# Attention with a gated MLP on one core: the table that sets the sequence of 2,462 steps is set anew

## The chip, the core and the metric

The kernel runs on one core of one Trainium2 chip. The core has TensorE (PE in the profile) for matrix products, VectorE (DVE), ScalarE (ACT) and GpSimd (POOL) for everything element by element, and SyncE (SP), which here only issues DMAs. Each engine works through its own list of instructions in order; semaphores hold an instruction until what it reads or overwrites is ready. The metric is the device time of one execution in microseconds (us), the median of several runs.

## The reference, cut to what matters

```
attention:  q, k, v are [4, 12, 448, 64]                       # batch, heads, tokens, width
    scores = q @ k.T / 8, causal mask, minus the row's maximum
    attn   = exp(scores) / (sum(exp(scores)) + 1e-9)
    x      = attn @ v, heads side by side                      # [4, 448, 768]
gated MLP, for each batch:
    h      = relu(x @ w_in)                                    # [448, 1024]
    u, v   = h[:, :512], h[:, 512:]
    v_n    = (v - mean(v)) / sqrt(var(v) + 1e-6)
    v_s    = w_spatial @ v_n + b_spatial                       # over the tokens
    out    = (u * v_s) @ w_out                                 # [448, 768]
```

w_in and w_out arrive as 64-bit floats, the other inputs as 32-bit floats.

## The kernel before, in words

**Tiling.** The 48 heads are taken two at a time: 24 pairs, six to a batch. Products that must be exact to more than 16 bits are made of three 16-bit products: every operand is split into a high part (`h`) and a low part (`l`), and a chain multiplies high by high, high by low and low by high.

**The steps.** For the first ten pairs ("wide" pairs) `qk_prepare` turns q and k on TensorE (L763 for pair 0, L789 for the others) into a PSUM bank, and ACT or DVE copies the bank to `qkT` (L772, L774, L810, L812). `wide` makes the scores in float32 (L979), DVE takes mask and row extreme in one step (L1017), ACT the exponential with its sum (L1027), DVE the reciprocal (L1038, L1046), one of POOL, ACT or DVE the scaling (`scaled_copy`: L496 is its form on DVE, L498 on ACT, L500 on POOL), TensorE turns the result (L1066) and ACT or DVE copies it (L1090, L1092). `attend` multiplies by v into the one bank `px` (L1300), and ACT and DVE take it out as high and low part of `xT` (L1317, L1322): until L1322 has read `px`, the next pair's L1300 waits. The other 14 pairs scale and split q and k first (L577 or L579 a sum of squares, on ACT or DVE; L623 its total on TensorE; L500 and L532 the split), are turned by DMA, and make their scores from 16-bit parts (L1146, L1147, then L1157, L1169, L1183, L1191, L1258).

**Weights.** `prep_in` and `prep_out` load w_in and w_out, turn 64-bit words into 32-bit floats on DVE in three steps (`from_double`: L1335, L1341, L1346), and split them (L500, L532). `v_load` loads v.

**The MLP.** `ffn` of a batch makes all its products in chains of three matmuls (L1544): v's half of h (`wi` by `xT`, four tiles of tokens), its evacuation (L1617), mean and variance (L1625, L1630, L1636, L1644 on POOL, L1651), the norm (L1661 on ACT or L1663 on POOL) and the split (`scaled_copy` and L1676) into `vn`; u's half (`xT` by `wi`); the spatial product (`wst` by `vn`), which needs `vn` of all four tiles; the gate (L1730, then L1564); and the output product (`wo` by `g`), evacuated by L496 or L498 and stored by L1782.

**What sets the order.** No scheduler runs. `Plan.add` collects 2,462 steps in program order, and three tables written into the file decide the rest: `ORDER` gives the sequence in which all steps are issued, and so each engine's list; `WHERE` gives the engine (A, P, D or S) of each step that can run on more than one; `FILLS` puts so many idle products (L714, 256 columns, into a bank that holds nothing) in front of a step on TensorE. Buffers are handed out in that sequence too, so that a buffer's number can differ while the work is the same. `Plan.run` also plays the sequence through with costs, for the length that it reports; these are not waits in the program. The lines of it that issue:

```python
for n in ORDER:
    op = self.ops[n]
    e = op.at_engine
    ...
    if e in op.lock:
        start = max(start, pool_end)
    if e == "POOL":
        start = max(start, dve_end)
    if e == "PE":
        last = op.cls
        if n in FILLS and (2, []) in free["pf"]:
            order += [(self.warm, e)] * FILLS[n]
    ...
    order.append((op, e))
```

Of the kernel before, what the change touches and what calls it, by code (L numbers as in the profile page):

```python
# [46 lines left out]
    15: 10, 17: 1, 19: 3, 21: 2, 158: 6, 160: 7,  # L47
# [4 lines left out]
    "AADAPPDAAPAPPPPPPAPPPPAADPAAPPDDAAPAAAAAPAAAPPADPAAAPAADDAPDPDDAAPDPPDADADAPADAADAADAAPDAAPPAAPPAAAAPDAAAAAPAP"  # L52
    "APAAAPAAPAADADDAAAAAPPAPPAAAAAAAAAPPADAAPAPAPPDAPPAADPPPPAAADPPAPPPPPADDAAAAAAAPPAAAADDPAPAPDAAADAAPPDDAAAAPAD"
    "DAPDAAADAADAAAAAAAPPAAPDSPDPAAAAAAPADAAAAAPAPAAPAPPAAAAAAPAAPSSAADDPPPPPPPAPPADAAPPAPAPDPPPAAADDAAAAAPPPPPPPPA"
    "AAPPPPAPDPAAAPPPPPPAAPADAPPDPPPAPAAPAPDDPDAPAAADAPPPDPPDAAAPAPPPPPAPPPADDAPPAPPPPPPDAADDAAAAAPPAAPPPPAAAPPADPS"
    "APAAPPPPPPSPPAAAPPPPPSAPADAPPPAPDAPPDDPADADPAAPPDADDDPPPAPDDAPADAAADAA"
)
ORDER = (
# [1788 lines left out]
```

## Time and profile before

| | us |
|---|---|
| median of 3 runs (lowest, highest) | 351.37 (351.15, 351.75) |
| the profiled execution: its time | 352.04 |
| its span, first to last instruction | 350.1 |
| TensorE busy, share of the span | 339.0, 97% |
| VectorE busy | 283.9, 81% |
| ScalarE busy | 273.5, 78% |
| GpSimd busy | 167.1, 48% |

The profile is one execution, in which every instruction has a start and a duration. Busy time of an engine is the union of its instructions' durations. Matmuls overlap: a matmul's duration is longer than the distance to the next one, so that the rate is read from the distance (a row of n matmuls, less one duration, divided by n - 1). A wait is the idle time of an engine in front of an instruction, put down to what ended last before it.

### The profile page before, as it was taken

To read this page: it belongs to the slowest core of one execution; us is meant where nothing else is said; L and a number is where in the kernel's file an instruction comes from. 1 tells how busy PE (TensorE), PEld (TensorE's weight loads), DVE (VectorE), ACT (ScalarE), POOL (GpSimd) and SP (SyncE) were. 2 spreads that over 40 slices of the span, in tenths; PEclk is the share of its full clock that TensorE was granted. 3 is DMA by queue.
4 is the path that set the end of the run, shared out by engine and by line. 5 is a ranking of instruction groups with operands and counts; after the bars stand their busy time and mean duration, and the time that the engine had idled before them with its cause. 6 is when DMAs were issued, how large, how long until landed. Compare 5 with 4: busy or idle time off the path is not lost.

```text
span 350.1 us, 8017 instructions
## 1 busy us (share of the span) xinstructions
PE 339.0 (97%) x2603; PEld 198.8 (57%) x2603; DVE 283.9 (81%) x1079; ACT 273.5 (78%) x747; POOL 167.1 (48%) x232
## 2 busy tenths in 40 slices
PE   7899998999999999999999999999999999999996
PEld 5556664655466565555565556654655665454563
DVE  4899999899999999997889988888999886263310
ACT  2798998999999999997997889899879676113112
POOL 3221962238535979662465665336788500033300
PEclk9999999999999999999999999999999999999999
DMA  7789938887876889998989979989887939500023
GB/s 176 167 223 215 278 69 210 213 197 203 161 180 172 146 170 180 180 206 186 178 192 181 173 158 176 228 187 185 130 128 146 162 81 166 153 2 0 2 87 93
DMA packets 160987, 55.49 MB, mean 158 GB/s; under 512 B 155249, under 2 KB 157106, under 8 KB 160946
## 3 DMA queue, kind: packets, MB, share of 16 engines
q1 hardware_dynamic: 160946, 54.99, 76.7%
q8 instruction: 20, 0.33, 0.4%
q14 instruction: 21, 0.17, 0.2%
HBM read 26.76 MB, written 5.51 MB: 92 GB/s over the span
## 4 chain that ended last, share of the span: by engine, by line
PE 46%; ACT 5%; DVE 5%; POOL 2%; issue 1%; ACTq 0%; DVEq 0%; POOLq 0%
PE pf L1544 37%; PE px L1300 5%; PE ps L1146 2%; PE ps L1147 2%; ACT ps L1169 2%; ACT junk L577 1%; DVE ps L1157 1%; DVE ln L1625 1%; ACT hv L1661 1%; POOL vn L1676 1%; ACT e L498 1%; DVE e L1258 1%; ACT hv L1617 0%; DVE junk L579 0%; ACT o L498 0%
## 5 line engine op out<-in xcount | busy, mean ns | idle before, releaser
L1544 PE MATMUL pf<-wi,xT 128*128 128x512 f16 (+1 forms) x360 | 62.4, 337 | 0.0
L1544 PE MATMUL pf<-xT,wi 128*128 128x448 f16 x288 | 59.5, 353 | 0.2 <-ACT hv L1617 0.2
L1169 ACT ACTIVATE ps<-ps,sm 128x384 f32<-128x384 f32 (+4 forms) x98 | 45.3, 464 | 10.0 <-DVE sm L1157 8.5
L1258 DVE SCALAR_TENSOR_TENSOR e<-ps,sm,e 128x256 f16<-128x256 f32 (+4 forms) x98 | 45.8, 505 | 5.4 <-ACT e L498 4.5
L1544 PE MATMUL pf<-wo,g 128*128 128x384 f16 x288 | 49.2, 326 | 0.2 <-ACT o L498 0.2
L1157 DVE CUSTOM_DVE_ANT_0 ps<-ps,mask,sc 128x256 f32<-128x256 f32 (+4 forms) x98 | 46.8, 507 | 1.5 <-ACT et L1090 0.2
L498 ACT ACTIVATE e<-ps,sm 128x256 f16<-128x256 f32 (+4 forms) x98 | 42.6, 509 | 3.3 <-DVE sm L1191 1.3
L532 POOL TENSOR_TENSOR qks<-qk,qks 112x512 f16<-112x512 f32 x28 | 33.5, 1204 | 20.1 <-DVE qks L496 10.6
L1544 PEld LDWEIGHTS <-wi 128*128 128x128 f16 x288 | 27.0, 98 | 27.0 <-issue 3.1
L1544 PEld LDWEIGHTS <-xT 128*128 128x128 f16 (+1 forms) x360 | 27.6, 102 | 23.7 <-issue 2.7
L1544 PEld LDWEIGHTS <-g 128*128 128x128 f16 (+1 forms) x288 | 27.7, 98 | 19.7 <-issue 1.1
L500 POOL TENSOR_SCALAR e<-e,sm 128x256 f32<-128x256 f32 (+3 forms) x33 | 17.1, 530 | 42.5 <-DVE sm L1046 13.5
L1027 ACT ACTIVATE e<-ps,sm 128x384 f32<-128x384 f32 (+3 forms) x70 | 34.2, 498 | 3.9 <-DVE sm L1017 2.3
L1544 PE MATMUL pf<-wst,vn 128*128 128x448 f16 (+1 forms) x176 | 35.6, 353 | 0.5 <-POOL vn L1676 0.5
L979 PE MATMUL ps<-qkT 64*128 64x256 f32 (+3 forms) x160 | 28.4, 446 | 2.1 <-ACT e L1027 1.6
L1544 PEld LDWEIGHTS <-vn 128*128 128x128 f16 (+1 forms) x176 | 16.6, 98 | 16.8 <-POOL vn L1676 1.4
L1644 POOL TENSOR_TENSOR ln<-ln,mhalf 128x1 f32<-128x1 f32 (+1 forms) x16 | 9.5, 591 | 34.8 <-DVE ln L1636 34.6
L1017 DVE CUSTOM_DVE_ANT_0 ps<-ps,e 128x128 f32<-128x128 f32 (+2 forms) x60 | 24.3, 448 | 2.1 <-PE ps L979 1.9
L1147 PE MATMUL ps<-qkT 128*64 128x256 f16 (+4 forms) x196 | 25.7, 285 | 0.0
L1066 PE MATMUL ps<-ident,e 128*128 128x128 f32 x160 | 24.1, 280 | 1.0 <-DVE e L496 0.6
L1146 PE MATMUL ps<-qkT 128*64 128x256 f16 (+4 forms) x196 | 24.2, 288 | 0.0
L1300 PE MATMUL px<-et,vs 128*64 128x448 f16 (+3 forms) x336 | 22.6, 275 | 0.1
(182 smaller groups left out, 710.1 us busy)
## 6 DMA issues: line engine op xcount, KB each, us to landing
wb<-in_moe_w_in_dram SPq DMA_DIRECT2D x12, 512.0 KB, 4.5
vnat<-in_v_dram SPq DMA_DIRECT2D x24, 192.0 KB, 4.2
out_dram<-o SPq DMA_DIRECT2D x9, 384.0 KB, 3.5
qk<-in_q_dram SPq DMA_DIRECT2D x14, 224.0 KB, 4.2
qk<-in_k_dram SPq DMA_DIRECT2D x14, 224.0 KB, 4.3
o<-in_moe_w_out_dram SPq DMA_DIRECT2D x8, 384.0 KB, 4.6
qk<-in_q_dram SPq DMA_DIRECT2D x20, 112.0 KB, 4.5
qk<-in_k_dram SPq DMA_DIRECT2D x20, 112.0 KB, 4.4
```

The source lines that it names most:

```text
L498: nc.scalar.activation(out=dst, in_=src, func=AF.Copy, scale=scale)
L532: lambda e: HANDLE[e].tensor_tensor(out=dst_l(), in0=src(), in1=dst_h(), op=ALU.subtract),
L979: nc.tensor.matmul(out=at(bank)[r0:r0 + rn, o0:o0 + n], lhsT=flat32(t)[rows, q0:q0 + rn], rhs=k32(t)[rows, :n], start=True, stop=True, ski ...
L1017: lambda e, ps=ps, n=n, u=u0 + u, sm=sm, o0=o0, h=h: nc.vector.tensor_tensor_reduce(out=at(ps)[:, o0:o0 + n], in0=at(ps)[:, o0:o0 + n], in ...
L1027: lambda e, ps=ps, n=n, u=u0 + u, sm=sm, o0=o0, c=c: nc.scalar.activation(out=at(eb)[:, 128 * c:128 * c + n], in_=at(ps)[:, o0:o0 + n], fu ...
L1146: nc.tensor.matmul(out=o, lhsT=w, rhs=qkT[:, 2 + x, :n], start=True, stop=False)
L1147: nc.tensor.matmul(out=o, lhsT=w, rhs=qkT[:, 4 + x, :n], start=False, stop=True)
L1157: lambda e, ps=ps, n=n, u=u, sm=sm, o0=o0, m0=m0: nc.vector.tensor_tensor_reduce(out=at(ps)[:, o0:o0 + n], in0=at(ps)[:, o0:o0 + n], in1=m ...
L1169: nc.scalar.activation(out=dst, in_=src, func=AF.Exp, scale=-1.0, bias=at(sm)[:, u:u + 1], accum_out=at(sm)[:, 4 + 2 * u:5 + 2 * u],)
L1258: lambda e, part=part, src=src, sm=sm, u=u: nc.vector.scalar_tensor_tensor(out=part(1), in0=src(), scalar=at(sm)[:, 12 + u:13 + u], in1=pa ...
L1300: nc.tensor.matmul(out=at(px)[64 * h:64 * h + 64, 128 * j:S], lhsT=lhsT, rhs=rhs, start=(j == 0 and t == 0), stop=(j == 3 and t == (0 if t ...
L1544: nc.tensor.matmul(out=o, lhsT=a(), rhs=rhs, start=(n0 + n == 0), stop=(n0 + n == len(mms) - 1), skip_group_check=len(out_ap()) > 1,)
```

## The change

Nothing but the three tables changes: the same steps, the same functions, another sequence, in places another engine, and other idle products.

```diff
 FILLS = {
-    15: 10, 17: 1, 19: 3, 21: 2, 158: 6, 160: 7,
+    15: 17, 21: 1, 99: 2, 159: 5, 160: 1,
 }
 WHERE = (
-    "AADAPPDAAPAPPPPPPAPPPPAADPAAPPDDAAPAAAAAPAAAPPADPAAAPAADDAPDPDDAAPDPPDADADAPADAADAADAAPDAAPPAAPPAAAAPDAAAAAPAP"
+    "AADAPPPAPPPPDPAPPAPAPPAAPADAPPDDPAPAPAAAPPAAPPADAAAAPADAPPDDPDDAAPPAPPAADAAPADDPAAAADDAPADAAPAAPADAPAAAAAAAAPAP"
 ...
 ORDER = (
-    0, 157, 7, 2, 6, 8, 9, 1, 79, 11, 13, 12, 3, 5, 15, 17, 16, 18, 19, 14, 21, 22, 10, 152, 4, 102, 20, 107, 103,
 ...
```

Steps 15, 17, 19 and 21 are the four turns of pair 0 (L763). Counted over the whole program, ScalarE has 531 instructions instead of 547, GpSimd 251 instead of 237, VectorE 1,082 instead of 1,081, and TensorE 26 idle products instead of 29. The largest moves are six norms (L1661 on ACT to L1663 on POOL), seven evacuations of the output (L498 to L496), and the three sums of squares of q and k that VectorE had (L579), which are all on ScalarE now (L577). The load of a q half of pair 1 now stands ahead of pair 0's four q and k loads, and two k halves of pair 1 stand between these and the first load of w_in.

Place one, the start of the program on VectorE. `ps` are the banks with pair 0's scores, `wb` is a piece of w_in as loaded, `wa` the piece as float. Before:

```order
L1017 ISA ps_76,sm_118<-ps_76,e_93 128x256
L1017 ISA sm_118 128x1
L1017 ISA ps_74,sm_119<-ps_74,e_93 128x384
L1017 ISA sm_119 128x1
L1335 TENSOR_SCALAR wa_142<-wb_144 128x512
L1017 ISA ps_73,sm_119<-ps_73,e_93 128x384
```

After:

```order
L1335 TENSOR_SCALAR wa_142<-wb_144 128x512
L1017 ISA ps_76,sm_118<-ps_76,e_93 128x256
L1017 ISA sm_118 128x1
L1017 ISA ps_74,sm_119<-ps_74,e_93 128x384
L1017 ISA sm_119 128x1
L1017 ISA ps_73,sm_119<-ps_73,e_93 128x384
```

The first step on w_in stood behind the fifth of pair 0's six minima and stands behind the third now.

Place two, the third and fourth pair. VectorE up to the step that reads `px` of the third pair (`xT_99`), before:

```order
L1341 SCALAR_TENSOR_TENSOR wa_142<-wb_144,wa_142 128x512
L1335 TENSOR_SCALAR wa_142<-wb_145 128x512
L1341 SCALAR_TENSOR_TENSOR woe<-o_111,woe 128x384
L496 TENSOR_SCALAR e_94<-e_94,sm_118 128x384
L1346 SCALAR_TENSOR_TENSOR wa_142<-wb_144,wa_142 128x512
L1341 SCALAR_TENSOR_TENSOR wa_142<-wb_145,wa_142 128x512
L1346 SCALAR_TENSOR_TENSOR woe<-o_111,woe 128x384
L1346 SCALAR_TENSOR_TENSOR wa_142<-wb_145,wa_142 128x512
L1322 SCALAR_TENSOR_TENSOR xT_99<-px_77,vsc_129,xT_99 128x448
```

After:

```order
L1341 SCALAR_TENSOR_TENSOR woe<-o_112,woe 128x384
L1335 TENSOR_SCALAR wa_142<-wb_144 128x512
L1335 TENSOR_SCALAR wa_142<-wb_145 128x512
L1341 SCALAR_TENSOR_TENSOR wa_142<-wb_145,wa_142 128x512
L1346 SCALAR_TENSOR_TENSOR wa_142<-wb_145,wa_142 128x512
L1038 TENSOR_REDUCE sm_119<-sm_119 128x1
L1341 SCALAR_TENSOR_TENSOR wa_142<-wb_144,wa_142 128x512
L1346 SCALAR_TENSOR_TENSOR wa_142<-wb_144,wa_142 128x512
L1046 RECIPROCAL sm_121<-sm_121 128x4
L1346 SCALAR_TENSOR_TENSOR woe<-o_112,woe 128x384
L1046 RECIPROCAL sm_119<-sm_119 128x1
L1322 SCALAR_TENSOR_TENSOR xT_99<-px_77,vsc_129,xT_99 128x448
```

The scaling L496 has left the row; the steps on weights have stayed. TensorE in the same place, from the third pair's L1300 to the fourth's, before (all of it):

```order
L1066 MATMUL ps_74<-ident,e_93 128x128 x3
L1066 MATMUL ps_75<-ident,e_94 128x128 x3
L1066 MATMUL ps_76<-ident,e_94 128x128 x3
L789 MATMUL ps_73<-ident,qk_82 128x112 x4
L979 MATMUL ps_74<-qkT_86 128x128
L979 MATMUL ps_75<-qkT_86 128x128
L979 MATMUL ps_74<-qkT_86 128x256
L979 MATMUL ps_75<-qkT_86 128x256
L979 MATMUL ps_76<-qkT_86 128x384
L979 MATMUL ps_73<-qkT_86 128x384
L1300 MATMUL px_77<-et_96,vnat_88 64x448 x2
```

After (its first rows; two more products with `xT_97`, three with `xT_98` and the same six L979 follow before L1300):

```order
L1066 MATMUL ps_73<-ident,e_94 128x128 x3
L1066 MATMUL ps_75<-ident,e_93 128x128 x3
L1066 MATMUL ps_76<-ident,e_93 128x128 x3
L1066 MATMUL ps_74<-ident,e_93 128x128 x4
L1066 MATMUL ps_73<-ident,e_93 128x128 x3
L789 MATMUL ps_75<-ident,qk_82 128x112 x4
L789 MATMUL ps_76<-ident,qk_82 128x112 x4
L789 MATMUL ps_74<-ident,qk_83 128x112 x4
L1544 LDWEIGHTS xT_97
L1544 MATMUL pf_78<-wi,xT_97 128x512
```

There are 7 more turns L1066, 8 more turns L789 and 6 more L1544 between the two.

Place three, GpSimd in the third batch's MLP. `vn_66` is the last of the four `vn` tiles to be made, `qks` belongs to later pairs. Before:

```order
L1644 TENSOR_TENSOR ln_131<-ln_131,mhalf 128x1
L500 TENSOR_SCALAR qks_84<-qk_83 112x8x64
L532 TENSOR_TENSOR qks_84<-qk_83,qks_84 112x8x64 x2
L500 TENSOR_SCALAR vn_117<-hv_113 128x512
L1676 TENSOR_TENSOR vn_117<-hv_113,vn_117 128x512
L1644 TENSOR_TENSOR ln_133<-ln_133,mhalf 64x1
L500 TENSOR_SCALAR qk_81<-qk_81,sc_125 112x512
L500 TENSOR_SCALAR vn_66<-hv_114 64x512 x2
L500 TENSOR_SCALAR vs_92<-vnat_89,vsc_130 128x8x64
L500 TENSOR_SCALAR qks_84<-qk_81 112x8x64
L500 TENSOR_SCALAR vs_91<-vnat_88,vsc_130 128x8x64
L1676 TENSOR_TENSOR vn_66<-hv_114,vn_66 64x512
```

After:

```order
L1663 TENSOR_SCALAR hv_113<-hv_113,ln_131 128x512
L500 TENSOR_SCALAR vn_115<-hv_113 128x512
L500 TENSOR_SCALAR qks_84<-qk_81 112x8x64 x2
L532 TENSOR_TENSOR qks_84<-qk_81,qks_84 112x8x64 x2
L893 COPY qkT_86<-qkT_86 64x896
L1644 TENSOR_TENSOR ln_132<-ln_132,mhalf 64x1
L1644 TENSOR_TENSOR ln_133<-ln_133,mhalf 128x1
L1663 TENSOR_SCALAR hv_114<-hv_114,ln_133 128x512
L1663 TENSOR_SCALAR hv_113<-hv_113,ln_132 64x512
L1676 TENSOR_TENSOR vn_117<-hv_114,vn_117 128x512
L500 TENSOR_SCALAR vn_66<-hv_113 64x512
L1676 TENSOR_TENSOR vn_66<-hv_113,vn_66 64x512
```

Two tiles' norms (L1663) and splits stand at the end of the row instead of one, and no other pair's work stands among them any more. On TensorE, 27 products of u's half follow the last product of v's half there before the spatial products begin, where 36 did.

## Rows read from the trace of the kernel before

**Rows 1.** The page, busy us, share of the span and instructions by engine.

```profile
PE 339.0 (97%) x2603; PEld 198.8 (57%) x2603; DVE 283.9 (81%) x1079; ACT 273.5 (78%) x747; POOL 167.1 (48%) x232
```

**Rows 2.** Windows: us, busy by engine (instructions), PEclk, DMA share, GB/s.

```profile
40.00:50.00 10.00, 9.41 (x70) 5.01 (x66) 9.93 (x29) 9.89 (x30) 8.59 (x11) 1.00 0.75 144
50.00:60.00 10.00, 9.03 (x67) 5.98 (x67) 9.90 (x31) 8.05 (x25) 1.42 (x2) 1.00 0.69 167
60.00:70.00 10.00, 9.87 (x78) 5.88 (x77) 8.86 (x32) 9.46 (x31) 3.50 (x7) 1.00 0.85 205
70.00:80.00 10.00, 10.00 (x72) 5.19 (x71) 9.81 (x39) 9.59 (x24) 4.61 (x7) 1.00 0.89 210
```

**Rows 3.** Waits of PE: who, waited for, us in total, times, longest us.

```profile
PE px L1300 <- DVE sm L1038: 0.9, 1, 0.9
...
PE pf L1544 <- POOL vn L1676: 0.5, 2, 0.3
...
PE px L623 <- DVE sm L1183: 0.3, 1, 0.3
...
PE pf L1544 <- ACT hv L1617: 0.2, 1, 0.2
```

**Rows 4.** Timeline, the start, PE: start us, us, what, idle before and releaser.

```profile
1.11 2.31 PE L714 MATMUL pf<-ones 128*128 128x256 f16 x10 [1.11 <-DVE ones L640]
4.39 0.93 PE L763 MATMUL ps<-ident,qk 112*64 112x112 f32 x4 [0.96 <-DMA qk<-in_q_dram]
...
8.77 2.40 PE L979 MATMUL ps<-qkT 64*128 64x128 f32 x12
...
14.09 0.82 PE L714 MATMUL pf<-ones 128*128 128x256 f16 x6
```

**Rows 5.** Timeline, the start, SP and DVE; last, the landing of that w_in load.

```profile
4.01 0.49 SPq L1369 DMA_DIRECT2D wb<-in_moe_w_in_dram  x1
...
11.54 0.43 DVE L1017 CUSTOM_DVE_ANT_0 ps<-ps,e 128x256 f32<-128x256 f32 x1
...
12.40 0.42 DVE L1335 TENSOR_SCALAR wa<-wb 128x512 int32<-128x512 int32 x1
...
DMA to landing us min/median/max: 6.5/6.5/6.5
```

**Rows 6.** Timeline, the third and fourth pair, POOL, DVE and PE.

```profile
47.13 1.16 POOL L532 TENSOR_TENSOR wi<-wa,wi 128x512 f16<-128x512 f32 x1 [0.92 <-ACT wi L498]
47.19 1.39 DVE L1335 TENSOR_SCALAR wa<-wb 128x512 int32<-128x512 int32 x1
...
49.68 1.25 POOL L532 TENSOR_TENSOR wi<-wa,wi 128x512 f16<-128x512 f32 x1
49.85 1.64 DVE L1346 SCALAR_TENSOR_TENSOR wa<-wb,wa 128x512 int32<-128x512 int32 x1
49.98 0.87 PE L1066 MATMUL ps<-ident,e 128*128 128x128 f32 x6 [0.58 <-DVE e L496]
50.69 0.55 PE L789 MATMUL ps<-ident,qk 112*128 112x112 f32 x4
...
52.48 0.68 DVE L1346 SCALAR_TENSOR_TENSOR wa<-wb,wa 128x512 int32<-128x512 int32 x1
53.08 0.67 DVE L1322 SCALAR_TENSOR_TENSOR xT<-px,vsc,xT 128x448 f16<-128x448 f32 x1
```

**Rows 7.** Timeline, the third batch's MLP, POOL, DVE, ACT and PE.

```profile
252.44 4.15 PE L1544 MATMUL pf<-xT,wi 128*128 128x448 f16 x21
...
252.81 0.47 ACT L1617 ACTIVATE hv<-pf,inv 64x256 f32<-64x256 f32 x1
...
254.08 3.03 POOL L532 TENSOR_TENSOR qks<-qk,qks 112x512 f16<-112x512 f32 x2
254.46 1.64 DVE L579 CUSTOM_DVE_ANT_0 junk<-qk 112x512 f16<-112x512 f32 x1
...
256.77 0.45 ACT L1617 ACTIVATE hv<-pf,inv 64x256 f32<-64x256 f32 x1
```

More of the change, by code (lines that the diff above doesn't have):

```diff
@@ L51 @@
 WHERE = (
-    "AADAPPDAAPAPPPPPPAPPPPAADPAAPPDDAAPAAAAAPAAAPPADPAAAPAADDAPDPDDAAPDPPDADADAPADAADAADAAPDAAPPAAPPAAAAPDAAAAAPAP"
[L53 to L56, printed above, removed]
+    "AADAPPPAPPPPDPAPPAPAPPAAPADAPPDDPAPAPAAAPPAAPPADAAAAPADAPPDDPDDAPPAPPAADAAPADDPAAAADDAPADAAPAAPADAPAAAAAAAAPAP"
+    "APAAPPDAPPAAPAAAAAAAPAAPAAAAAAAPDAAPAAAAAAPAPPDAAPPPPPPPPAADAAPPPPPPPPDDAAAAAAAAPAAPPAAADDAPADDPDAAAAAAAAPDPAA"
+    "DAPAAPAADPADAAAAAPAPPAPSDPAPAAAAADPAADPAAAPAPPPPAPPDAAAAADDAPSSPPPDPPPPPPPPDPAADAAPAPPPAPADAADDDADDAAADPPPPDSA"
+    "AAPPPPPPPAPAAPPPAPPDPPAADPPAPPPDAAAAAPAPPDAPAAAAAAPPDPPDPPDPPAPPPDPPAPDAAAAPPPPPDPPDADDADAAAAPPAPPAPAAAAPPPDDP"
+    "PAAAPPPAPPAPAAAPPPPPPSAPAAPPPDPPPPPAPPPDPPAPPDPPDDDDAPDDPPPDPPDDADAADD"
 )
 ORDER = (
[125 rows of a table removed]
[125 rows of a table added]
     2424, 2425, 2426, 2427, 2428, 2434,
```

249 rows, old and new, of the table ORDER are left out of this document.

## The prediction

> **What bounds the kernel now.** Read first the page's line of engines: TensorE is busy 339.0 of 350.1 us [rows 1], so nearly all of the span is matmuls, which this change leaves as they are, three idle products apart. A gain can come only from TensorE's idle time and from products that run slower than elsewhere. Next come the windows: TensorE is busy 9.41 and 9.03 of 10 us from 40 to 60, and 9.87 and 10.00 in the two windows behind [rows 2]. In 40 to 60 that is 1.56 us lost, against 0.13 in 60 to 80, and in the same two windows VectorE is busy 9.93 and 9.90. Then the list of waits says for whom TensorE waited [rows 3]: 0.9 us in front of L1300, 0.5 us in two waits for `vn`, 0.3 for the total at L623, 0.2 for `hv`. The timeline shows the start [rows 4, 5], the third and fourth pair [rows 6] and the third batch's MLP [rows 7], three stretches in which the change moves work and TensorE stands or is slow.
>
> **The start: 0, between -1.0 and +1.0 us.** Ten idle products run from 1.11 for 2.31 us, then TensorE idles 0.96 us for pair 0's q and starts its turns at 4.39 [rows 4]. These ten take 0.23 us each; the six at 14.09 take 0.14 each [rows 4], so the clock granted at the start is the lower of the two levels. Seven more idle products at 0.21 to 0.23 us last 1.5 to 1.6, so the seventeen end at about 4.9 to 5.0. One q load of pair 1 is now issued ahead of pair 0's, and one load takes SP 0.5 us (the w_in load: 0.49 [rows 5]), so pair 0's q lands near 4.39 + 0.5 = 4.9. The fillers then cover the idle time exactly and delay nothing; what would be late without them is that load. Should the clock rise sooner because TensorE no longer stands in front of the turns, sixteen turns (four of them take 0.93 us, [rows 4]) could each be up to 0.1 us shorter, 1.6 us together.
>
> I do not book that, because the next thing is late instead: the first piece of w_in. Its load is issued at 4.01 and lands 6.5 us later, at 10.5; VectorE comes to L1335 at 12.40, so today it waits for nothing [rows 5]. After, two more loads stand ahead of it on SP: issue about 4.01 + 2 x 0.5 = 5.0, landing about 11.5. L1335 has moved in front of the fourth minimum of pair 0, which starts at 11.54 today [rows 5], so VectorE can't pass 11.5 there however early pair 0's scores are. Behind it come L1335 itself (0.42), the fourth minimum (0.43) and the fifth, and the sixth minimum starts where it does today to within 0.2 us. If the load lands as soon as before, up to 1 us of the shorter turns gets through; if it lands 1 us later still, VectorE and behind it the exponential and TensorE's next scores are 1 us late. I take 0: the two gains and losses meet at one DMA, and its only row has the landing at the place where VectorE arrives.
>
> **The third and fourth pair: -1.3 us.** Two of VectorE's weight steps are slow here: L1335 takes 1.39 us from 47.19, 0.06 us after GpSimd's L532 had begun, and L1346 takes 1.64 us from 49.85, also begun under an L532 (49.68); the same L1335 elsewhere takes 0.42 [rows 5] and the same L1346 0.68 [rows 6]. That is 0.97 + 0.96 us that VectorE stands. Behind it L496 is late and TensorE's turns L1066 wait 0.58 us; then L1322, at 53.08 and last in VectorE's row, frees `px` late, and the fourth pair's L1300 waits 0.9 us [rows 3, 6].
>
> After, L496 has left this stretch (another engine scales `e`), so the 0.58 goes. For `px`, TensorE gets more to do between the two L1300: 7 more turns L1066 (0.87/6 = 0.145 each at most [rows 6]), 8 more L789 (0.55/4 = 0.14 each), 6 more L1544 (21 of them take 4.15, so 0.2 each [rows 7]): 1.0 + 1.1 + 1.2 = 3.3 us at most, some 2.8 if a row's drawn-out last matmul is taken off. VectorE's row before L1322 gains two L1335 and two L1341 and loses others, some 1 us net. 2.8 less 1 is more than the 0.9 that is waited, so the wait goes if VectorE's steps keep their usual length, and half of it stays if one port wait stays. I take -0.7 of the 0.9 and -0.6 for L1066, between 0 and -1.5.
>
> **The third batch's MLP: -0.5 us, between -0.5 and +3.5.** VectorE's L579 on `qk` takes 1.64 us from 254.46 beside two L532 of GpSimd from 254.08, 3.03 us together [rows 7]; its total at L623 makes TensorE wait 0.3 us, and 0.2 us go to `hv` (L1617) [rows 3]. The change gives all three sums of squares of q and k to ScalarE, off that port, and sets the two halves of the last L1617, 4 us apart before (252.81 and 256.77 [rows 7]), side by side. Both waits go. What is late next is `vn_66`, the last operand of the spatial products: two norms (L1663) and their splits now stand at the end of GpSimd's row, and TensorE's cover is 27 products of u's half instead of 36, 9 x 0.2 = 1.8 us less. I hold that the 4 us from L1617 pay for both; the third rival is that they don't.
>
> **Other waits: -0.3 and +0.6.** Of the 0.5 us for `vn` [rows 3] I take 0.3 off, for the last batch, where GpSimd's row ahead of `vn` is shorter. A sequence of 2,462 steps set anew has small waits at new places; the listed ones behind the fourth pair (0.5, 0.3 and 0.2) are 1.0 us [rows 3], and I add 0.6. Fourteen more instructions on GpSimd, at 167.1/232 = 0.72 us each [rows 1], are 10 us on an engine that is idle half the time: nothing by themselves, but ten more microseconds in which a VectorE step can meet them.
>
> **The sum.** 0 - 0.6 - 0.7 - 0.5 - 0.3 + 0.6 = -1.5 us against the profiled execution's 352.04, so 350.5; that execution lies 0.67 above the median, so **349.9** as a median.
>
> **Rivals.** First, the start gains after all: w_in lands at 10.5 as before, or earlier, VectorE isn't held and 1.0 us of the shorter turns arrives: 348.9. For it speaks that the two k loads ahead are small; against it that SP issues one load at a time [rows 5].
>
> Second, the port waits are only laid elsewhere. In [rows 6] both slow steps begin 0.06 and 0.17 us after an L532, and both stand until it is over. If in the new sequence an L532 begins as often just ahead of VectorE's steps on weights, the -0.6 and -0.7 stay away: -0.2 in the sum, 351.2. The Trainium skill says the same as a rule (page "SBUF — State Buffer", section "SBUF: two separate sides"): the pair of ports that VectorE and GpSimd share is an exclusive lock, whichever starts first has it for its whole instruction, and the other blocks fully. That rule speaks against this change in that GpSimd gets more instructions, each of which can be first; the trace agrees, by the 0.97 and 0.96 us in [rows 6]. For the change speaks that two of the steps that met the port (L496, L579) are gone from the two stretches.
>
> Third, on the other side, one mechanism: `vn_66`. If the path from v's last product over the evacuation, the statistics, two norms and the splits on GpSimd to `vn_66` is longer than TensorE's cover, TensorE stands in front of the spatial products. The cover is 1.8 us shorter, and GpSimd has 1.8 us more ahead of `vn_66` (two norms and two splits more at 0.72, less one of the other pairs' steps): between 1.8 and 3.6 us, less what L1617 gives back; I take 2.6. It decides from the point at which the path is over 11 us long, and today's took more. With the third batch's -0.5 not gained it makes -1.5 + 0.5 + 2.6 = +1.6, and with a half-gained third pair 353.0 as a median. Against it stands the row of L1617: the 3.96 us between its halves were on this path.
>
> **How the numbers follow.** A measurement here can tell about 0.2 %, 0.7 us, from no change. The forecast of 349.9 has a chance of 0.48, its own range is 349.0 to 350.8 (start ±1.0 not at once with the third pair's ends). The start's gain, 348.9: 0.13. Laid elsewhere, 351.2: 0.21. `vn_66`, 353.0: 0.18. Faster by over 0.2 % is below 350.7: nearly all of the first two less the forecast's upper edge, and a little of the third, 0.55. Within 0.2 %, 350.7 to 352.1: most of the third and that edge, 0.25. Slower: the fourth and what lies beyond my reading, 0.20. The range of 348.4 to 352.9 leaves out the lower end of the first rival and the upper half of the last.
>
> **What the changed profile would show.** Right: no idle TensorE between the fillers and L763, and VectorE idle in front of its first L1335 until about 11.5; L1335 and L1346 at 0.4 and 0.7 us in 40 to 55; no wait of TensorE at the fourth pair's L1300 and none for L496; no VectorE step of 1.6 us beside L532 near 254; the third batch's spatial products without a wait on `vn`. Wrong: a sixth minimum well before 12.7 (first rival), L1335 or L1346 again over 1.3 us beside an L532 (second), a wait of over 1 us of L1544 on GpSimd's L1676 near 260 (third). A wait of over 1 us at a place that I don't name would make the prediction wrong as a whole.

## The result, and the profile after

The changed kernel takes **354.8 us** (median, 353.94 to 354.94), the kernel before 351.22 us beside it (350.84 to 351.75): a ratio of 1.0089, 95% interval 1.0074 to 1.0104. The forecast was 349.9, its range 348.4 to 352.9: a gain was forecast and a loss came, outside the range. The span of the profiled execution is 353.1 us.

The page's line of engines answers to [rows 1]:

```profile
PE 340.7 (97%) x2600; PEld 196.3 (56%) x2600; DVE 288.3 (82%) x1080; ACT 262.9 (74%) x733; POOL 178.2 (50%) x246
```

TensorE is busy 1.7 us longer with three idle products fewer, so part of its work ran slower; ScalarE has 11 us less, GpSimd 11 us more. The waits of TensorE answer to [rows 3] (who, waited for, us in total, times, longest us):

```profile
PE ps L789 <- DMA qk<-in_q_dram: 2.8, 1, 2.8
PE px L623 <- ACT junk L577: 1.4, 1, 1.4
...
PE ps L1146 <- DVE e L1258: 1.1, 2, 0.6
PE px L623 <- ACT ps L1169: 0.8, 1, 0.8
PE px L1300 <- DVE xT L1322: 0.4, 1, 0.4
```

The longest wait stands at a place that the prediction does not name: pair 1's first turn L789, for a load of q. TensorE's timeline of the start shows it, beside [rows 4]:

```profile
1.11 3.81 PE L714 MATMUL pf<-ones 128*128 128x256 f16 x17 [1.11 <-DVE ones L640]
5.05 1.82 PE L763 MATMUL ps<-ident,qk 112*64 112x112 f32 x12
...
7.33 2.26 PE L979 MATMUL ps<-qkT 64*128 64x128 f32 x12
12.36 0.98 PE L789 MATMUL ps<-ident,qk 112*128 112x112 f32 x4 [2.77 <-DMA qk<-in_q_dram]
```

The first part went as forecast: 17 idle products, then twelve of pair 0's turns in 1.82 us (0.15 each, against 0.93 for four before), and the scores begin at 7.33 instead of 8.77. Then TensorE stands 2.77 us. In the kernel before, TensorE has the last of pair 0's scores there, ahead of pair 1's turns, and waits for ScalarE, not for a load:

```profile
12.25 0.97 PE L979 MATMUL ps<-qkT 64*64 64x448 f32 x4 [1.09 <-ACT e L1027]
13.15 1.10 PE L789 MATMUL ps<-ident,qk 112*128 112x112 f32 x8
```

Windows of the changed kernel (us, busy by engine (instructions), PEclk, DMA share, GB/s) show what follows:

```profile
10.00:11.00 1.00, 0.00 (x0) 0.00 (x0) 0.00 (x0) 0.28 (x2) 0.00 (x0) 1.00 1.06 340
11.00:12.00 1.00, 0.00 (x0) 0.00 (x0) 0.22 (x1) 0.00 (x0) 0.00 (x0) 0.99 1.29 234
12.00:13.00 1.00, 0.64 (x4) 0.67 (x5) 1.00 (x6) 0.30 (x2) 0.00 (x0) 0.50 1.29 175
...
18.00:19.00 1.00, 1.00 (x7) 0.50 (x6) 1.00 (x7) 0.01 (x1) 0.00 (x0) 0.59 1.23 278
19.00:20.00 1.00, 1.00 (x6) 0.36 (x5) 1.00 (x5) 0.98 (x5) 0.44 (x1) 1.00 0.48 102
```

TensorE stands from 9.59 us. The granted clock (PEclk, as a share of the higher level) is still 1.0 from 10 to 11, falls to 0.50 (the lower of its two levels, 1.2 GHz) just before 12 us, and is back at 1.0 from about 18.8, after TensorE had worked again since 12.36. In these 6.8 us products took nearly twice as long: the twelve L979 that begin at 14.61 last 3.33 us, in e4 below, at the higher level, 1.82.

In the first microseconds the column shows 1.00 too, but the trace holds no record of the clock there: its records begin at 5.2 us in the changed kernel and at 9.8 in the kernel before. Up to about these times the rows run at the lower rate (an idle product 0.22 to 0.23 us, against 0.11 in e4 below). So the change did bring the higher level forward; the start lost the gain again behind it.

In the middle of the program the windows that answer to [rows 2] are better, and three of the four later ones shown are worse (TensorE busy in the kernel before, in the order of the last four: 9.98, 9.47, 9.82 and 10.00):

```profile
40.00:50.00 10.00, 9.59 (x71) 5.18 (x70) 9.01 (x38) 9.10 (x27) 7.82 (x12) 1.00 0.94 248
50.00:60.00 10.00, 10.00 (x77) 6.55 (x76) 9.62 (x30) 9.48 (x29) 4.28 (x7) 1.00 0.63 176
...
190.00:200.00 10.00, 9.23 (x86) 5.24 (x84) 8.68 (x32) 8.03 (x20) 5.00 (x7) 1.00 0.87 170
250.00:260.00 10.00, 10.00 (x84) 5.64 (x82) 9.82 (x40) 7.68 (x25) 8.85 (x11) 1.00 0.79 170
260.00:270.00 10.00, 8.57 (x81) 5.11 (x80) 8.64 (x33) 7.45 (x20) 8.51 (x12) 1.00 0.75 144
270.00:280.00 10.00, 9.52 (x86) 5.74 (x84) 9.86 (x31) 6.68 (x19) 4.84 (x7) 1.00 0.74 106
```

### The profile page after: what moved, and what is told of

Same layout as the page of the kernel before. It is cut to its first block, busy times and chain, and to the rows that moved or that the text cites. A ratio compares the mean times of both kernels' runs of the same rounds, so it can differ in the third digit from the quotient of the medians.

```text
span 353.1 us, 8011 instructions
## 1 busy us (share of the span) xinstructions
PE 340.7 (97%) x2600; PEld 196.3 (56%) x2600; DVE 288.3 (82%) x1080; ACT 262.9 (74%) x733; POOL 178.2 (50%) x246
## 4 chain that ended last, share of the span: by engine, by line
PE 44%; DVE 18%; ACT 17%; DMA 8%; POOL 5%; issue 5%; SPq 2%; ACTq 0%; POOLq 0%; DVEq 0%
PE pf L1544 29%; PE px L1300 5%; DVE ps L1157 4%; ACT e L498 4%; ACT e L1027 4%; PE ps L979 3%; ACT ps L1169 3%; DVE e L1258 3%; DMA et<-e 2%; PE ps L1066 2%; DMA qk<-in_q_dram 2%; PE ps L1146 2%; ACT et L1090 1%; SPq L726 1%; PE ps L1147 1%
## 5 line engine op out<-in xcount | busy, mean ns | idle before, releaser
L1544 PE MATMUL pf<-wi,xT 128*128 128x512 f16 (+1 forms) x360 | 61.8, 337 | 0.0
L1544 PE MATMUL pf<-xT,wi 128*128 128x448 f16 x288 | 59.4, 353 | 0.0
L1169 ACT ACTIVATE ps<-ps,sm 128x256 f32<-128x256 f32 (+4 forms) x98 | 45.3, 463 | 12.9 <-DVE sm L1157 11.6
L1544 PE MATMUL pf<-wo,g 128*128 128x384 f16 x288 | 49.1, 326 | 0.0
L1258 DVE SCALAR_TENSOR_TENSOR e<-ps,sm,e 128x384 f16<-128x384 f32 (+4 forms) x98 | 45.8, 503 | 4.0 <-ACT e L498 3.4
L1157 DVE CUSTOM_DVE_ANT_0 ps<-ps,mask,sc 128x256 f32<-128x256 f32 (+4 forms) x98 | 46.3, 505 | 1.7 <-PE ps L1147 0.8
L498 ACT ACTIVATE e<-ps,sm 128x384 f16<-128x384 f32 (+4 forms) x98 | 43.0, 506 | 4.9 <-issue 1.7
L1544 PEld LDWEIGHTS <-wi 128*128 128x128 f16 x288 | 27.2, 98 | 25.8 <-issue 1.6
L1544 PEld LDWEIGHTS <-xT 128*128 128x128 f16 (+1 forms) x360 | 27.5, 102 | 23.7 <-issue 3.1
L500 POOL TENSOR_SCALAR e<-e,sm 128x256 f32<-128x256 f32 (+3 forms) x38 | 20.0, 535 | 38.0 <-DVE sm L1046 20.3
L1027 ACT ACTIVATE e<-ps,sm 128x384 f32<-128x384 f32 (+3 forms) x70 | 34.3, 501 | 6.5 <-DVE sm L1017 5.4
L1544 PEld LDWEIGHTS <-g 128*128 128x128 f16 (+1 forms) x288 | 27.5, 98 | 18.9 <-issue 0.4
L1544 PE MATMUL pf<-wst,vn 128*128 128x448 f16 (+1 forms) x176 | 36.1, 352 | 0.0
L532 POOL TENSOR_TENSOR qks<-qk,qks 112x512 f16<-112x512 f32 x26 | 31.1, 1203 | 7.8 <-ACT qks L498 6.6
L979 PE MATMUL ps<-qkT 64*128 64x256 f32 (+3 forms) x160 | 30.5, 467 | 0.2 <-ACT e L1027 0.2
L1544 PEld LDWEIGHTS <-vn 128*128 128x128 f16 (+1 forms) x176 | 16.8, 98 | 15.9 <-issue 0.6
L1146 PE MATMUL ps<-qkT 128*64 128x256 f16 (+4 forms) x196 | 24.1, 289 | 1.1 <-DVE e L1258 1.1
L498 ACT ACTIVATE o<-pf,oi 128x384 f32<-128x384 f32 x14 | 8.2, 590 | 22.4 <-PE pf L1544 22.4
L1066 PE MATMUL ps<-ident,e 128*128 128x128 f32 x160 | 23.3, 279 | 0.2
```

What stands on the lines that cost most here:

```text
L498: nc.scalar.activation(out=dst, in_=src, func=AF.Copy, scale=scale)
L532: lambda e: HANDLE[e].tensor_tensor(out=dst_l(), in0=src(), in1=dst_h(), op=ALU.subtract),
L979: nc.tensor.matmul(out=at(bank)[r0:r0 + rn, o0:o0 + n], lhsT=flat32(t)[rows, q0:q0 + rn], rhs=k32(t)[rows, :n], start=True, stop=True, ski ...
L1027: lambda e, ps=ps, n=n, u=u0 + u, sm=sm, o0=o0, c=c: nc.scalar.activation(out=at(eb)[:, 128 * c:128 * c + n], in_=at(ps)[:, o0:o0 + n], fu ...
L1066: nc.tensor.transpose(out=at(pt)[:, 128 * i:128 * i + 128], in_=e32(at(eb))[:, c0 + i, :], identity=ident)
L1146: nc.tensor.matmul(out=o, lhsT=w, rhs=qkT[:, 2 + x, :n], start=True, stop=False)
```

## The experiments

Each kernel was timed beside the kernel before on the same chip, so that the ratio is what to compare. The last column counts executions whose mean granted clock was 0.995 or less; a mean of 0.99 over 353 us is 7 us at half the clock, 0.995 is 3.5 us. A profile is of one execution only: those of e1 and e2 are of executions whose clock stayed up, those of e3 and e7 of the one whose clock fell.

| kernel | us | before | ratio, 95% interval | clock 0.995 or less |
|---|---|---|---|---|
| changed | 354.80 | 351.22 | 1.0089 [1.0074, 1.0104] | 5 of 5 |
| e1_load | 354.62 | 351.83 | 1.0070 [1.0045, 1.0095] | 5 of 6 |
| e2_dve | 353.45 | 351.83 | 1.0052 [1.0033, 1.0070] | 8 of 12 |
| e3_both | 351.75 | 351.83 | 1.0004 [0.9991, 1.0017] | 1 of 12 |
| e4_fill | 353.44 | 351.83 | 1.0046 [1.0032, 1.0060] | 0 of 5 |
| e5_after_start | 354.29 | 351.56 | 1.0082 [1.0053, 1.0111] | 5 of 6 |
| e6_before_start | 351.55 | 351.56 | 1.0003 [0.9989, 1.0016] | 0 of 12 |
| e7_third | 351.59 | 351.56 | 1.0008 [0.9992, 1.0023] | 1 of 12 |
| e8_fill17 | 350.14 | 351.56 | 0.9963 [0.9951, 0.9974] | 0 of 12 |
| e9_l856 | 351.57 | 351.76 | 0.9997 [0.9984, 1.0009] | 0 of 12 |
| e10_sum | 350.45 | 351.76 | 0.9966 [0.9954, 0.9978] | 0 of 5 |
| e11_oldfills | 354.27 | 351.76 | 1.0079 [1.0059, 1.0099] | 1 of 6 |
| e12_l496 | 351.20 | 351.76 | 0.9988 [0.9978, 0.9998] | 0 of 12 |
| e13_l579 | 350.04 | 351.16 | 0.9959 [0.9944, 0.9974] | 0 of 9 |
| e14_two | 349.77 | 351.16 | 0.9956 [0.9939, 0.9973] | 0 of 7 |
| e15_two579 | 350.08 | 351.52 | 0.9958 [0.9944, 0.9973] | 0 of 6 |

The kernel before had none below 0.999 beside e1 to e15. In e1, e2, e3 and e5 to e7 the table of the sequence is written on six lines fewer, so their lines in a profile are six lower (L783 is L789).

### Which half of the program loses

The first 155 steps of both sequences, to about 24 us, are the same steps but for two, so that they can be exchanged. In short (this is not the file's own text):

```diff
-order = ORDER_BEFORE
+head = ORDER_CHANGED[:155]
+order = head + [n for n in ORDER_BEFORE if n not in head]     # e5; e6 the other way round
```

> The first 155 steps (to about 24 us), their engines and the idle products of the changed kernel, then everything else as in the kernel before; the two sets of 155 steps differ in two steps. Start theory (the whole loss is made before 24 us): slower than the kernel before by 2 to 3.5 us, with a mean granted clock of 0.99 to 0.995: 353.5 to 355.3. Spread theory (the loss is also made in many small waits after it): 352 to 353.

> The other half of the pair: the first 155 steps, their engines and the idle products of the kernel before, then everything else as in the changed kernel. Start theory: granted clock 1.0 in every execution, and the rest of the change is worth nothing in sum (1.4 us won from 40 to 60 us, about as much lost near 190 and 262): 351.8 within 0.6. Spread theory: 353 or more. If the gain from 40 to 60 us were whole: 350.5.

The changed start alone costs 0.82% (2.7 us), with the low clock in five of six executions; the rest of the change alone is 1.0003. The start theory holds: the loss is made before 24 us, and the rest of the change is worth nothing that can be told in sum (interval -0.11% to +0.16%).

### What in the start loses: a load, VectorE's place, the clock

SP's queue of the changed kernel, in the timeline (start us, us issuing):

```profile
5.08 0.49 SPq L1369 DMA_DIRECT2D wb<-in_moe_w_in_dram  x1
5.62 0.43 SPq L726 DMA_DIRECT2D qk<-in_q_dram  x1
```

The w_in load lands 6.7 us after its issue, at 11.8, and the q load issued behind it, with 112 KB against 512 KB, 6.6 us after its own, at 12.2. The views of these two loads' lines, w_in first:

```profile
DMA to landing us min/median/max: 6.7/6.7/6.7
...
who waited for it (us, times):
  PE ps L789: 2.8, 1
...
DMA to landing us min/median/max: 6.6/6.6/6.6
```

VectorE stands as well, up to its L1335 for that w_in load; the sixth of pair 0's minima starts at 12.98, in the kernel before at 12.74 (timeline; last the row of the kernel before):

```profile
11.78 0.43 DVE L1335 TENSOR_SCALAR wa<-wb 128x512 int32<-128x512 int32 x1 [2.20 <-DMA wb<-in_moe_w_in_dram]
...
12.98 0.60 DVE L1017 CUSTOM_DVE_ANT_0 ps<-ps,e 128x384 f32<-128x384 f32 x1
...
12.74 0.56 DVE L1017 CUSTOM_DVE_ANT_0 ps<-ps,e 128x384 f32<-128x384 f32 x1
```

In the sequence the two moves are (a part of the table; the 73 behind it is taken out):

```diff
-    109, 27, 28, 112, 113, 115, 105, 117, 29,        # 27 loads w_in, 28 is L1335
+    109, 73, 27, 28, 112, 113, 115, 105, 117, 29,    # e1: 73, pair 1's q load, first
+    109, 27, 112, 113, 115, 105, 117, 28, 29,        # e2: L1335 behind 117, the sixth minimum
+    109, 73, 27, 112, 113, 115, 105, 117, 28, 29,    # e3: both
```

> The changed kernel with one step moved: the q load of pair 1 (step 73) is issued ahead of the first w_in load instead of behind it. In the changed kernel it was issued at 5.62 us and landed at 12.23, right behind w_in (11.76). Load theory (TensorE's 2.77 us of idle time in front of L789 and the low clock behind it come from this load): it lands near 7.8, no idle time over 1 us there, granted clock stays at the higher level, 354.8 - 2.6 = about 352.2 us. VectorE theory (what counts is that VectorE stands in front of L1335 for w_in with three minima behind it): w_in now lands 0.5 us later, near 12.2, banks come free as late as before, and TensorE stands at the next turn instead: 354.8 or 0.5 more. Clock theory (the wait itself costs nothing against the kernel before, the low clock behind it costs 2 to 3 us): the time follows the clock; if idle time stays long at another place, no gain.

> The changed kernel with one step moved: the first L1335 stands behind the fifth of pair 0's minima again (as in the kernel before), the loads as in the changed kernel. VectorE theory: minima four and five come 2.2 us earlier, at 9.6 and 10.0, banks come free, and 1.5 to 2.5 us are gained: about 352.8. Load theory: TensorE's next instruction still waits for the q load until 12.3, the clock falls as before, 354.8 within 0.4.

> Both moves of the two kernels above. Load theory: as with the load alone, 352.2 within 0.4. VectorE theory: as with VectorE alone or better, 352.8. If each hides the other (TensorE needs the load and the banks), only this kernel gains, and more than the two alone together: 351.5 to 352.

In e2 and e3 L1335 stands behind all six minima, not behind the fifth as the expectation has it: 117 is the sixth, and in the kernel before L1335 stands ahead of it. So VectorE has one minimum more ahead of w_in than there.

Alone, the load gives 0.19% and VectorE's place 0.37% of the changed kernel's 0.89%; together they give 0.85%, nearly all of it. The interval of e1 overlaps that of the changed kernel, so that the load alone can't be told from nothing. With the load alone it lands after 2.7 us, and TensorE then stands 0.74 and 1.75 us in front of two turns for ScalarE's L1027, which waits for the minima behind L1335; with VectorE alone it stands 1.82 us for the load (e1, its load's landing, then e2; L783 is L789, L1021 is L1027; the view of the landing takes in the k load issued just ahead of q):

```profile
12.78 0.60 PE L783 MATMUL ps<-ident,qk 112*128 112x112 f32 x4 [1.75 <-ACT e L1021]
...
DMA to landing us min/median/max: 2.7/2.8/2.9
...
12.02 0.57 PE L783 MATMUL ps<-ident,qk 112*128 112x112 f32 x4 [1.82 <-DMA qk<-in_q_dram]
```

Neither the load theory nor the VectorE theory holds by itself: each hides the other. The single executions say more than the medians: e1's one with the clock up took 352.13, its others 353.88 to 355.35; e2's four with the clock up 351.87 to 352.57, the others 353.29 to 355.07.

So the clock was tested by itself, with the load and VectorE left as they are:

```diff
-    15: 17, 21: 1, 99: 2, 159: 5, 160: 1,
+    15: 17, 21: 1, 97: 26, 99: 2, 159: 5, 160: 1,    # 97 is the turn that waits
```

> The changed kernel with 26 idle products (0.11 us each, 2.8 us) in front of the turn L789 that waits for the q load; nothing else is touched. Clock theory: TensorE's wait becomes busy time of the same length, the granted clock stays at the higher level from 12 to 18.6 us where it was at half, and 2 to 3 us are gained although nothing lands earlier: 352 to 352.8. Load theory without the clock, or VectorE theory: the same work waits for the same data, 354.8 within 0.4.

TensorE's timeline and a window of this kernel:

```profile
9.78 3.01 PE L714 MATMUL pf<-ones 128*128 128x256 f16 x26
12.69 0.57 PE L789 MATMUL ps<-ident,qk 112*128 112x112 f32 x4
```

```profile
12.00:13.00 1.00, 1.00 (x11) 0.81 (x9) 1.00 (x4) 0.08 (x1) 0.00 (x0) 1.00 1.14 178
```

The turn begins 0.3 us later than in the changed kernel and takes 0.57 us instead of 0.98; the clock stays up in all five executions, and the ratio falls from 1.0089 to 1.0046. That is 0.43%, 1.5 us, below the 2 to 3 that the clock theory expected and more than the 0.4 that the other two allowed. Of the loss of some 3 us about half is thus the low clock, and the other half is there at the full clock, with the late load and the held minima in place; e3 shows that it goes with these two.

### What the idle products do

```diff
 FILLS = {
-    15: 10, 17: 1, 19: 3, 21: 2, 158: 6, 160: 7,
+    15: 17, 21: 1, 158: 6, 160: 7,                       # e8, in the kernel before
```

> The kernel before with the changed kernel's idle products in front of pair 0's turns alone (17 ahead of the first and 1 ahead of the last, instead of 10, 1, 3 and 2); sequence and engines as before. Theory of the fillers: the turns run at the higher clock from 5 us, pair 0's scores end 1.5 us earlier, and since no load has moved and the minima are not held, 0.8 to 1.5 us arrive: 350.3 to 351. Rival: TensorE only stands longer in front of its next product (for ScalarE's exponential or pair 1's loads, which land after 10.7 us), 351.8 within 0.3, or the clock falls in that longer idle time, 353 to 355.

TensorE and VectorE in the start of e8:

```profile
4.71 1.03 PE L763 MATMUL ps<-ident,qk 112*64 112x112 f32 x8
...
7.02 2.26 PE L979 MATMUL ps<-qkT 64*128 64x128 f32 x12
10.02 0.97 PE L979 MATMUL ps<-qkT 64*64 64x448 f32 x4 [0.74 <-ACT e L1027]
...
10.17 0.42 DVE L1335 TENSOR_SCALAR wa<-wb 128x512 int32<-128x512 int32 x1
10.51 0.56 DVE L1017 CUSTOM_DVE_ANT_0 ps<-ps,e 128x384 f32<-128x384 f32 x1
```

These two entries of one line of the change win 0.37%, 1.4 us, inside the 0.8 to 1.5 us expected: the scores begin 1.75 us before those of [rows 4], VectorE reaches L1335 without standing, the sixth minimum is 2.2 us earlier than 12.74, and TensorE's next idle time is 0.74 us. Two things are in it that this run doesn't separate: the turns run faster (eight in 1.03 us, against 0.93 for four), and one idle product stands between them instead of six, some 1.2 us less. In the changed sequence the same products bring TensorE as early to a turn whose load is not there. The reverse, the old idle products in the changed sequence:

> The changed kernel with the idle products of the kernel before (10, 1, 3 and 2 in front of pair 0's turns, 6 and 7 later); sequence and engines as changed. Clock theory: TensorE comes 1.5 us later to the turn that waits for pair 1's q load at 12.3, stands there 1.0 to 1.3 us instead of 2.8, the clock stays up in most executions, and the kernel gets faster although its turns are slower: 352.8 to 353.5. Theory that the clock falls for the load whatever the idle time: 354.8 within 0.5. Theory that fillers help here too: over 355.

The clock stays up in five of six executions, as expected, but the time does not follow: 1.0079, no different from the changed kernel's 1.0089 within the intervals. TensorE stands 1.46 us for pair 0's q, its turns run at the lower clock, and L789 still waits 1.09 and 0.39 us for ScalarE's L1027. The expected 352.8 to 353.5 was wrong: the clock that stays up does not show in the time, and the scores begin at 9.26 instead of 7.33. That the late turns take what the clock gives back fits, but no run separates the two.

### The third and fourth pair

In short:

```diff
-step 444 (the third pair's scaling of e): VectorE, L496
+step 444: ScalarE, L498                                     # e12, in the kernel before
```

> The kernel before with one scaling of the third pair's e (L496 on VectorE at 49.4 us, for which TensorE waited 0.58 us) on ScalarE, as in the changed kernel; nothing else. As predicted for this term: the 0.58 us go and px comes 0.5 us earlier, 350.6 to 351.0. Rival: ScalarE, busy 9.89 of 10 us there, has it later than VectorE, TensorE waits as long or longer: 351.5 to 352.5.

0.9988, 0.56 us, at the edge of what can be told. TensorE's waits in e12:

```profile
PE ps L1066 <- ACT e L498: 0.8, 1, 0.8
...
PE px L1300 <- DVE sm L1038: 0.4, 1, 0.4
```

The wait for the scaling did not go; it went over to ScalarE and is 0.2 us longer, as the rival said. What is won is half of the wait for `px`. In the changed kernel the wait for the scaling is gone, and the fourth pair's L1300 (at 56.04) doesn't wait; the third pair's does:

```profile
47.74 2.10 PE L1300 MATMUL px<-et,vnat 128*64 128x448 f32 x16 [0.41 <-DVE xT L1322]
```

There the other engines' rows had moved too.

### The third batch's MLP

The rows of the changed kernel's ScalarE, then VectorE, GpSimd and TensorE, beside [rows 7]:

```profile
258.40 0.62 ACT L577 ACTIVATE junk<-qk 112x512 f16<-112x512 f32 x1
...
259.01 1.39 ACT L498 ACTIVATE e<-ps,sm 128x128 f16<-128x128 f32 x3
260.43 0.95 ACT L889 ACTIVATE qkT<-qkT 64x896 f16<-64x896 f16 x1
261.40 0.63 ACT L577 ACTIVATE junk<-qk 112x512 f16<-112x512 f32 x1
...
252.35 1.31 DVE L856 SCALAR_TENSOR_TENSOR sc<-sc 128x1 int32<-128x1 int32 x1
...
252.89 0.77 POOL L1663 TENSOR_SCALAR hv<-hv,ln 128x512 f32<-128x512 f32 x1
...
262.17 0.16 PE L623 MATMUL px<-sc,ones 128*128 128x2 bf16 x1 [1.43 <-ACT junk L577]
```

L579 with its 1.64 us is gone from VectorE, as forecast, but its sum of squares is now the last of ScalarE's row (261.40), and TensorE waits 1.43 us for it. Three ways to take it away were tried: the step moved ahead of the scalings; VectorE's L856, which takes 1.31 us here, moved behind the L1183 for which ScalarE's scalings wait; the sum put back on VectorE. The numbers are steps, the dots stand for steps left out:

```diff
-    2170, 1787, 2061, ..., 2045, 2072, 2171,      # 2170 and 2171 are the two L577
+    2170, 2171, 1787, 2061, ..., 2045, 2072,      # e7, on e3; e13: 2171 here, but L579 on VectorE
-    2037, 1774, ..., 2067,                        # 2037 is L856
+    1774, ..., 2067, 2037,                        # e9, on e6; e10 and e13 have it too
```

> The kernel with both moves at the start (load ahead of w_in, L1335 behind the fifth minimum; 351.75 us), and one more: in the third batch's MLP the second sum of squares of the last pair (L577 on ScalarE, at 261.4 us) stands directly behind the first (258.9) instead of behind three scalings L498 and a copy. ScalarE theory (TensorE's 1.4 us at L623 is ScalarE's row alone, made by giving it VectorE's sum of squares): the wait goes, 1.0 to 1.4 us are gained, 350.4 to 350.8. Rival: the scalings and the copy that now come 0.8 us later, or the norms on GpSimd, are waited for next: 351.5 to 351.8.

> The kernel with the start of before and the rest of the changed kernel (351.55 us), with one step moved on VectorE: the small step L856 (at 252.35 us in the changed kernel, 1.31 us long beside GpSimd's L500 and L1663, 0.14 to 0.21 us elsewhere) stands behind the three L1183 that followed it. Port theory (that one stalled step delays ScalarE's row by 1.3 us, and this row ends at the L577 for which TensorE waits 1.4 us at L623): ScalarE's scalings start near 252.8 instead of 254.0, the wait goes, 350.3 within 0.3. ScalarE theory (the row is too long without it): the wait stays over 0.8 us, 351.3 to 351.8. L856 may stall as long at its new place; that alone costs nothing.

> The kernel just named, and the changed kernel's idle products in front of pair 0's turns (17 and 1 instead of 10, 1, 3, 2), which gave 1.4 us in the kernel before. If the two gains are independent: 1.4 us under the kernel just named, 348.9 by the port theory, 350.1 by the ScalarE theory. If the sequence behind 24 us gives the start's gain back: 350.3 to 351.5.

> The sum kernel (start of before, 17 idle products first, rest as changed, L856 moved; 350.45 us) with the second sum of squares of the last pair back on VectorE (L579 instead of L577), behind L1322. ScalarE theory (TensorE's 1.1 us at L623 is there because ScalarE got VectorE's sum of squares): the wait falls to 0.3 or less, 0.7 to 1.0 us are gained, 349.5 to 349.8. Port theory (VectorE loses there as much, by L579 of 1.6 us beside L532 as in the kernel before, or GpSimd's norms come late behind it): wait over 0.8 us or a new wait for vn, 350.2 to 350.9.

Neither of the first two moved the time. In e7 the wait at L623 went and the next product waited as long, for the copy that now came behind it on ScalarE (TensorE's timeline; L883 is L889):

```profile
261.15 0.22 PE L1141 MATMUL ps<-qkT 128*64 128x64 f16 x1 [1.32 <-ACT qkT L883]
```

In e9 the wait at L623 fell only from 1.4 to 1.1 us. That doesn't clear the port theory: L856 takes 0.91 us at its new place as well, and ScalarE waits a little later for the L1157 that stands behind it (VectorE, then ScalarE in e9):

```profile
249.95 0.91 DVE L856 SCALAR_TENSOR_TENSOR sc<-sc 128x1 int32<-128x1 int32 x1
...
252.09 0.61 ACT L1169 ACTIVATE ps<-ps,sm 128x448 f32<-128x448 f32 x1 [0.57 <-DVE sm L1157]
```

So the long step was moved and not removed, and what it costs in all isn't shown. Nor is it 0.14 to 0.21 us in all other places, as the expectation says: three of its 14 in the changed kernel take 0.8 to 1.3 us. e10 has e9's sequence and e8's idle products: 0.9966 against 0.9997, 0.31% of e8's 0.37%. Its 350.45 us lies 0.35 over the 350.1 of independent gains and just inside the other range, and the intervals don't tell a gain that arrives whole from one that arrives in part. In e13, with the sum on VectorE, the waits are

```profile
PE pf L1544 <- POOL vn L1676: 0.5, 1, 0.5
...
PE px L623 <- DVE ln L1636: 0.2, 1, 0.2
```

and the time is 0.9959 against e10's 0.9966: 0.2 us at L623 instead of 1.1, but 0.5 us more for `vn`, and no difference that the intervals can tell. The sum on ScalarE made that wait; putting it back takes the wait away but not its length off the time.

> The last kernel with one more sum of squares back on VectorE: the second of the pair for which TensorE waits 0.8 to 1.4 us at L623 near 194 us (L579 instead of L577; VectorE stands 0.75 us there). ScalarE theory: that wait goes too, ScalarE's L1169 behind it come 0.8 us earlier, 0.7 to 1.1 us gained, 349.0 to 349.4. Rival (as at the third batch's MLP, the wait goes and another takes its place): 349.8 to 350.2.

The second sum of squares, near 190 us, did nothing that can be told (0.9958 against e13's 0.9959): TensorE still waits there,

```profile
190.50 0.16 PE L623 MATMUL px<-sc,ones 128*128 128x2 bf16 x1 [1.04 <-DVE xT L1322]
```

and the releaser is now named: L623 writes `px`, and L1322 reads the pair before out of it until 190.44. In e13 and in the changed kernel L1322 also ends 0.06 us before this L623 begins, though their rows put the wait down to ScalarE, whose instruction ended last there. The wait at 262.17 is another matter: there L1322 had ended 2 us before, and it went with the sum (e7, e13).

### Two parts together

> The kernel before with two parts of the change alone: the 17 idle products first (1.4 us gained alone) and the scaling of the third pair on ScalarE (0.56 gained alone). If independent: 351.7 - 1.4 - 0.56 = 349.7. If the earlier start takes the second gain away: 350.1 to 350.3.

e14_two is e8 with e12's edit, and at 349.77 us (0.9956) the fastest median of all. It meets the 349.7 of independent gains only in microseconds: the kernel before beside it took 351.16, not 351.7, and by the ratio the second gain is not seen on top of the first (e8's 0.9963 lies inside the interval). It is not excluded either. e8, e10 and e13 to e15 all beat the kernel before by 0.34 to 0.44%, and can't be told from one another.

## Why the prediction was wrong, point by point

**The start, forecast 0 between -1.0 and +1.0: +2.7 (e5).** This is the step that failed. Its rows were read rightly as far as they were read: the idle time in front of L763 is gone, w_in lands at 11.8 (forecast 11.5), VectorE stands until then, and the sixth minimum starts at 12.98, 0.24 us later than before (forecast within 0.2). But the working followed one load and one engine only. It counted what was put ahead of the w_in load on SP and did not ask what stands behind it: pair 1's next q load, issued at 5.62 us, lands behind w_in's 512 KB, as it did before, but 1.5 us later than the 10.7 there. And it kept TensorE's next step from the kernel before, where the last of pair 0's scores come ahead of pair 1's turns; in the changed sequence the turn comes first, and it needs that load. "The two gains and losses meet at one DMA" was right for VectorE. For TensorE, which had become 1.6 us earlier, the same landing was 2.77 us of standing, and then the clock. The prediction weighed the clock as a gain only; that it can fall again after a longer idle time was in no case, and it is half of the loss (e4). That the clock may rise sooner, which it named and did not book, came; e8 shows that this part of the change gains 1.4 us where the loads are left alone.

**The third and fourth pair, forecast -1.3.** Near in size: TensorE's windows from 40 to 60 gain 1.15 us (19.59 against 18.44). The slow steps are gone, as forecast: from 40 to 55 no L1335 takes more than 0.43 us and no L1346 more than 0.69. But a wait for `px` stands one pair earlier, 0.41 us at 47.74, and the removal of L496, for which 0.6 was booked, doesn't take its wait away by itself (e12). The size is in part luck.

**The third batch's MLP, forecast -0.5, up to +3.5.** Wrong in sign, though inside its own range: from 250 to 280 TensorE is busy 28.09 us, against 29.29. The prediction let both waits go and named `vn_66` as what is late next; TensorE didn't wait for `vn` at all. What was late was ScalarE, to which one of the three sums of squares taken "off that port" had gone here. The step "both waits go" looked at the engine that lost the work and not at the one that got it.

**Other waits, forecast -0.3 and +0.6.** The -0.3 came (320 to 330: 10.00 against 9.67). The new waits are larger than the 0.6: 0.75 us from 190 to 200 alone. In sum the rest is 1.0003 (e6): what is won in one place is lost again in others. TensorE's waits behind 24 us in e6's profile are L623 1.4 and 0.8 us, L1146 1.1 in two and L1300 0.4, 3.7 together; in the kernel before the same list adds up to 3.2.

**The rivals.** The first, the start's gain gets through, happens when the loads are left as they were: e8, 350.14 us. The second, port waits laid elsewhere, is partly seen: its signs, L1335 or L1346 over 1.3 us, did not come (the longest on w_in take 0.58 and 0.69), but L856 takes 1.31 us beside GpSimd; what that costs TensorE isn't shown (e9). The third had the right sign and the wrong place; its 353.0 is the sum without the half-gained third pair that it names, with which it would be 353.6.

What stays open is why the changed rest gives back the gain of 40 to 60 us. Four edits went against its waits (e7, e9, e13, e15); two took one away, and each time another stood in its place; the other two left it, and the time stayed. The 1.1 us at L1146, two waits for VectorE's L1258, was left alone in all of them.

## What to carry to other kernels

When a resequencing makes one engine earlier, list what it needs next in the new order and where each of those loads stands in its queue, the large one ahead of it included; an engine that arrives early at a load only stands there, and for TensorE standing cost a second time here, through the clock. Test a table of many moves by halves: two exchanges of the first 155 steps separated a loss of 2.7 us from a rest worth nothing, and two entries of one line of the change, alone, were a gain of 0.4%. A wait that went when one engine's row was shortened stood in front of the next product or for another engine (e7, e13), so a wait's length in a list is not what its removal wins.

## What the runs showed of the hardware

**Idle time and the clock.** The clock fell in more of a kernel's executions where TensorE's longest idle time between 9 and 13 us was longer in its profile: 2.77 us (changed), 5 of 5 executions; 2.07 (e5), 5 of 6; 1.82 (e2), 8 of 12; 1.75 (e1), 5 of 6; 1.09 and 1.08 (before, e9), none; 1.09 (e11), 1 of 6; 0.74 (e6, e8), none of 12 each; 0.74 there and 1.24 or 1.01 near 16 us (e3, e7), 1 of 12 each; filled with idle products (e4), none of 5. It is no fixed outcome: the same kernel had both, and the profiles with 1.82 and 1.75 us are of executions whose clock stayed up. In the profiled execution of the changed kernel the lower level lasted 6.8 us, in e5's, with the clock down from 11.9 to 15.3, half that. In the changed kernel, idle products that only filled a wait for a load were worth 1.5 us (e4).

**Idle products at the start.** The clock's records begin at 3.8 to 7.1 us in the profiles of the twelve kernels with 17 idle products in a row at the start, and at 7.5 to 10.2 us in those of the five with ten; until about then the rows run at the lower rate.

**A small load behind a large one.** In the start a load of 112 KB issued 0.54 us behind one of 512 KB landed 0.5 us behind it, after 6.6 us; issued ahead of it (e1), after 2.7 us. The large one itself took 5.3 us (e1) to 6.9 (e4) in the profiles of the changed starts.

**A small VectorE step beside GpSimd.** L856, 128x1, 0.18 us in the median of its 14, started at 252.35, while GpSimd's L500 ran until 252.89, and ended at 253.66, as L1663 did, which followed L500 without a gap. It started before L1663 and yet ended only with it; in e9, at its new place, it ended with the same L1663 again, after 0.91 us. That GpSimd held it is argued from these ends.
